# The first batch of an inducing-point attention and hard-swish kernel: a split first load, more input tiles in flight, weights cast while they are loaded, and a hand-written order for the first batch's coefficients

## The chip, the cores and the metric

One NeuronCore of a Trainium2 chip runs the kernel. Its engines are TensorE (PE, with its weight loads shown apart as PEld), VectorE (DVE), ScalarE (ACT), GpSimd (POOL) and SyncE (SP); SP and POOL issue the DMA transfers here. The metric is the device time of one execution in microseconds (us); lower is better. Executions of this kernel agree within about half a per cent.

## The reference

Four batches of N = 12480 tokens with C = 128 channels first meet m = 32 inducing points, then the tokens attend back, and the result runs through a two-layer block with a hard-swish.

```python
def mab(q, kv):
    s = scale * (q @ kv.transpose(0, 2, 1))
    s = s - s.max(-1, keepdims=True)
    a = np.exp(s)
    a /= a.sum(-1, keepdims=True) + 1e-09
    return a @ kv
h = mab(I, x)                    # 32 rows for each batch
x = mab(x, h).reshape(B * N, C)  # 49920 tokens
h = x @ w_in                     # d_ff = 2048
g = h * np.clip(h + 3.0, 0.0, 6.0) / 6.0
out = g @ w_out                  # float32, 49920 x 128
```

## The kernel before

The kernel never forms the 2048-wide hidden layer for each token. A token after the second attention is a weighted mean of the 32 rows of H (the `h` above), with weights that sum to one. As long as no entry of H @ w_in exceeds 3 in size, the hard-swish is a quadratic, and the square of a weighted mean is the weighted mean of the squares less a sum over pairs of rows: weight of m times weight of n times the squared difference. So each batch needs 32 x 128 linear coefficients (`L`, spread over a block-diagonal tile `BD`) and 512 x 128 pair coefficients (`Cq`), and each token needs its 32 exponentials and the 512 products of two of them. A counter at the end checks that the shortcut held; otherwise a slow direct path runs.

The tokens of a batch are cut into seven groups: six of 2048 (128 partitions with 16 tokens each, 1 MB) and a last one of 192 (48 partitions with 4 tokens). A group has four chunks of 512 tokens, the last group one, so a batch has 25 chunks.

The work of a batch has three stages, named by the first letter of the functions.

Stage a gathers H: `load_x` brings a group in from DRAM on the POOL queue (float32 for the matmuls, tiles `xr`, four of them), `a_cast` makes a bf16 copy `xb` on ACT and DVE, `a_T` transposes it on PE into `pt` in two halves and DVE copies each half to `xT`, `a_s1` computes the scores `s` and ACT takes the exponential `a`, `a_agg` adds a'x into one PSUM bank `hnd` and DVE adds `a` into `dacc`. At the end of a group's `a_agg` the load of the group four further on is issued, and for the first batch the load of the two weight matrices goes out after that of its last group.

Stage c makes the coefficients: `c_sum` and `c_den` reduce `dacc` and normalise `hnd` to H, `c_HT` transposes H and forms the differences `dH` and sums `W`, `c_sq` squares dH'w_in in 16 blocks, `c_C` multiplies these with w_out into `cp`, `c_G`, `c_hs`, `c_L` and `c_BD` make the linear part, and `c_tail` copies `cp` to `Cq`. Both need w_in and w_out in bf16 as well as in float32: before the change w_in is cast in two halves on ACT (lines 630 and 637) and w_out is scaled by -1/6 on DVE (line 641).

Stage b works on chunks. `b_pack` and `b_e` make a group's exponentials, `b_spread` copies rows of `dk` across partitions with a DMA on the SP queue into `d`, `b_base` and `b_prod` make the pair terms `TF` and `TD`, `b_f` and `b_r` the normaliser, `b_lin` and `b_quad` multiply with `BD` and `Cq` into `op`, and `b_evac` scales to `os`, from which SP writes the output.

Every engine works through its instructions in the order in which the program writes them. That order is written by hand: the loop over chunks (lines 666 to 714) emits stage b of chunk t and prepares chunks t+1 to t+5; between its pieces `bg` takes units of stages a and c of the next batch from a queue at an even rate. The first batch has nothing to hide behind: `a_first` emits its stage a (lines 291 to 308), then the first units of stage c with filler matmuls (`warm`) between them, and the rest of stage c runs in five steps of the loop with t below zero, beside the preparation of the first chunks.

```python
queue = c_units(0)
...
n_units, span = len(queue), (LEAD + 3)
begin = -LEAD - 3
for t in range(-LEAD - 3, total):
```

Of the kernel before, what the change touches and what calls it, by code (L numbers as in the profile page):

```python
# [9 lines left out]
FP32 = mybir.dt.float32  # L10
FP32R = mybir.dt.float32r
BF16 = mybir.dt.bfloat16
# [14 lines left out]
XBUF = 4  # L27
# [12 lines left out]
def kernel(  # L40
# [38 lines left out]
    with ExitStack() as es:  # L79
# [3 lines left out]
        xin = es.enter_context(tc.tile_pool(name="xin", bufs=XBUF))  # L83
        xbin = es.enter_context(tc.tile_pool(name="xbin", bufs=2))
# [20 lines left out]
        def load_x(b, g):  # L105
            t0, p, n = groups[g]
            src = x[b, t0 : t0 + p * n, :].rearrange("(p i) c -> p i c", i=n)
            t = xin.tile([P, TG, C], FP32R, name="xr")
            nc.gpsimd.dma_start(t[:p, :n, :], src)  # L109
            xs[(b, g)] = t  # L110
        for g in range(XBUF):
            load_x(0, g)
# [6 lines left out]
        ones = const.tile([P, P], FP32, name="ones")  # L119
        nc.vector.memset(ones[:, :], 1.0)  # L120
        blk_f = const.tile([P, P], FP32, name="blk_f")
        nc.vector.memset(blk_f[:, :], 0.0)
        one4_f = const.tile([P, SL], FP32, name="one4_f")
        nc.vector.memset(one4_f[:, :], 0.0)
        for q in range(4):
            nc.vector.memset(blk_f[32 * q : 32 * q + 32, 32 * q : 32 * q + 32], 1.0)
            nc.vector.memset(one4_f[32 * q : 32 * q + 32, q : q + 1], -1.0)
        blk = const.tile([P, P], FP32R, name="blk")
        nc.vector.tensor_copy(blk[:, :], blk_f[:, :])
        one4 = const.tile([P, SL], FP32R, name="one4")  # L130
        nc.vector.tensor_copy(one4[:, :], one4_f[:, :])
# [3 lines left out]
        nc.vector.tensor_copy(sel[:, :, :], ident[:M, :M].unsqueeze(1).to_broadcast([M, 4, M]))  # L135
        sel = sel[:, :, :].rearrange("k q m -> k (q m)")


        i_of = const.tile([P, 1], I32, name="i_of")
        nc.gpsimd.iota(i_of[:, :], pattern=[[0, 1]], base=0, channel_multiplier=1)  # L140
        nc.vector.tensor_single_scalar(i_of[:, :], i_of[:, :], 3, op=ALU.bitwise_and)
        half_of = const.tile([P, 1], FP32, name="half_of")
        nc.vector.tensor_copy(half_of[:, :], i_of[:, :])
# [86 lines left out]
        def a_agg(b, g, h, a1):  # L230
# [665 lines left out]
```

## Time and profile before

| | |
|---|---|
| Time, median of 3 runs | 333.91 us (332.82 to 334.44) |
| Profiled execution, own time | 333.31 us |
| Its span, from the first to the last recorded instruction | 331.5 us |
| PE busy | 300.7 us (91% of the span) |
| DVE, ACT, POOL busy | 242.1, 228.2, 17.7 us |
| Mean granted TensorE clock | 0.98 |
| HBM read, written | 27.67 MB, 25.56 MB |

The page gives one profiled execution, times in microseconds from the span's start. A busy PE is not PE at its peak, because matmuls are pipelined. Each row of a group of instructions names the line, the engine, the operation, what it writes and reads, the shapes and the count, then its busy time and the mean of one in ns, then the idle time ahead of it and what ended that. In the timeline the columns are start, duration (of all instructions in a merged row), engine, line and names. In the chain of waits, work is followed back from the last instruction to what released it. In a table of stretches each engine has its busy time and count, then the granted clock (1.00 is full), the share of time that the DMA engines were busy and the rate in GB/s.

### The profile page before, as it was taken

Reading aid. Unit: us, or ns where it says so; the run is one execution under the profiler, and the core shown is the slowest. Engines: PE = TensorE matmul, PEld = TensorE weight load, DVE = VectorE, ACT = ScalarE, POOL = GpSimd, SP = SyncE. Lnnn points to the kernel's source line nnn. Section 1 sums busy time; section 2 is a strip of 40 time slices with the busy share of each in tenths; the row PEclk is TensorE's granted clock in tenths of the full one; section 3 lists DMA queues with packets and bytes.
Section 4 is the critical chain, followed back from the end, with each engine's and each line's share of the span. In section 5 each row is a group of like instructions: output and inputs, shape, how many; then the busy total and the mean of one; then the engine's idle time right before and its main releaser. Section 6 shows DMA issues by size and latency. Waiting matters only on the chain.

```text
span 331.5 us, 9598 instructions
## 1 busy us (share of the span) xinstructions
PE 300.7 (91%) x3926; PEld 236.3 (71%) x3926; DVE 242.1 (73%) x560; ACT 228.2 (69%) x412; POOL 17.7 (5%) x37
## 2 busy tenths in 40 slices
PE   0868878999999998999999998999999999999970
PEld 0757456888767786888767886888767787777760
DVE  4765757778786866877795866878795867887980
ACT  2442459888579758888479758888479656777720
POOL 3031100001100000010100000010000000000000
PEclk9998979999999999999999999999999999999996
DMA  7699930378895455478994446473644356666561
GB/s 257 253 320 329 371 72 18 81 223 288 292 397 182 129 167 183 109 237 289 318 398 146 102 164 198 130 235 133 187 162 162 73 167 189 189 219 205 192 243 42
DMA packets 24134, 66.73 MB, mean 201 GB/s; under 512 B 3056, under 2 KB 17424, under 8 KB 17808
## 3 DMA queue, kind: packets, MB, share of 16 engines
q1 hardware_dynamic: 18160, 38.36, 35.7%
q0 software_dynamic: 5920, 27.66, 25.9%
q8 instruction: 33, 0.54, 0.7%
q14 instruction: 21, 0.17, 0.1%
HBM read 27.67 MB, written 25.56 MB: 161 GB/s over the span
## 4 chain that ended last, share of the span: by engine, by line
PE 80%; DVE 8%; ACT 5%; issue 2%; DMA 2%; POOL 1%; POOLq 0%; DVEq 0%
PE op L591 27%; PE bp L551 12%; PE hnd L235 7%; PE op L575 6%; PE pt L213 6%; PE dpm L414 4%; PE cp L434 4%; PE s L221 3%; PE pp L522 2%; DVE xT L214 2%; DMA xr<-in_x_dram 2%; PE sp L492 2%; PE lp L388 1%; PE ep L478 1%; ACT xb L204 1%
## 5 line engine op out<-in xcount | busy, mean ns | idle before, releaser
L558 ACT ACTIVATE TF<-bp 128x512 bf16<-128x512 f32 (+1 forms) x200 | 118.7, 601 | 35.0 <-PE rp L511 18.2
L591 PE MATMUL op<-Cq,TF 128*128 128x128 bf16 (+1 forms) x800 | 109.7, 223 | 0.2 <-DVE Cq L447 0.2
L591 PE MATMUL op<-Cq,TD 128*128 128x128 bf16 (+1 forms) x800 | 106.5, 219 | 0.0
L607 DVE TENSOR_TENSOR os<-op,r_all 128x512 f32<-128x512 f32 (+1 forms) x100 | 68.3, 683 | 21.0 <-PE op L591 19.9
L551 PE MATMUL bp<-xT,W 128*128 128x512 bf16 (+1 forms) x200 | 75.1, 376 | 0.0
L591 PEld LDWEIGHTS <-TF 128*128 128x128 bf16 (+1 forms) x800 | 50.4, 98 | 34.0 <-issue 25.5
L567 DVE TENSOR_TENSOR TD<-TF,d 128x1024 bf16<-128x1024 bf16 (+1 forms) x100 | 66.8, 668 | 3.9 <-ACT TF L558 2.1
L591 PEld LDWEIGHTS <-TD 128*128 128x128 bf16 (+1 forms) x800 | 61.5, 98 | 0.2 <-issue 0.2
L575 PE MATMUL op<-BD,nf 128*128 128x512 f32 (+1 forms) x100 | 52.9, 529 | 0.0
L204 ACT CAST xb<-xr 128x1024 bf16<-128x1024 f32 (+1 forms) x49 | 46.5, 957 | 8.0 <-DMA xr<-in_x_dram 7.8
L214 DVE COPY xT<-pt 128x1024 bf16<-128x1024 bf16 (+1 forms) x56 | 34.3, 618 | 12.2 <-PE pt L213 12.0
L425 ACT ACTIVATE sq<-dpm 128x512 bf16<-128x512 f32 x60 | 36.2, 651 | 6.0 <-PE dpm L414 5.9
L235 PE MATMUL hnd<-xr,a 128*32 128x128 f32 (+1 forms) x400 | 35.5, 231 | 1.7 <-ACT a L227 1.6
L213 PE MATMUL pt<-ident_b,xb 128*128 128x128 bf16 (+1 forms) x400 | 33.0, 229 | 4.1 <-DVE xb L204 4.1
L512 DVE RECIPROCAL r_all<-rp 128x4 f32<-128x4 f32 (+1 forms) x100 | 17.7, 177 | 23.0 <-PE rp L511 22.8
L511 PE MATMUL rp<-one,nf 128*128 128x4 f32 (+1 forms) x100 | 34.5, 345 | 0.0
L227 ACT ACTIVATE a<-s 128x512 fp32r<-128x512 f32 (+1 forms) x28 | 15.4, 551 | 22.4 <-PE s L221 17.7
L235 PEld LDWEIGHTS hnd<-xr,a 128*32 128x32 f32 (+1 forms) x400 | 27.1, 112 | 4.8 <-ACT a L227 2.9
L213 PEld LDWEIGHTS <-xb 128*128 128x128 bf16 (+1 forms) x400 | 25.7, 103 | 6.4 <-DVE xb L204 4.2
L109 POOL DMA_DIRECT2D xr<-in_x_dram x28 | 15.1, 542 | 205.2 <-PE bp L551 135.1
L434 PE MATMUL cp<-w6n,sq 128*128 128x128 bf16 x256 | 24.4, 220 | 1.0 <-DVE BD L408 1.0
L414 PE MATMUL dpm<-dH,w_in_b 128*128 128x512 bf16 x64 | 24.1, 389 | 0.9 <-ACT w_in_b L637 0.6
(99 smaller groups left out, 333.4 us busy)
## 6 DMA issues: line engine op xcount, KB each, us to landing
xr<-in_x_dram POOLq DMA_DIRECT2D x24, 1024.0 KB, 6.7
out_dram<-os SPq DMA_DIRECT2D x24, 1024.0 KB, 4.1
d<-dk SPq DMA_DIRECT2D x96, 128.0 KB, 3.9
w_in_r<-in_moe_w_in_dram POOLq DMA_DIRECT2D x1, 1024.0 KB, 6.1
w_out_r<-in_moe_w_out_dram POOLq DMA_DIRECT2D x1, 1024.0 KB, 10.2
xr<-in_x_dram POOLq DMA_DIRECT2D x4, 96.0 KB, 5.4
out_dram<-os SPq DMA_DIRECT2D x4, 96.0 KB, 1.9
d<-dk SPq DMA_DIRECT2D x4, 48.0 KB, 3.9
```

Of the source, the lines that this page charges most:

```text
L204: eng(xb[:p, lo:hi, :], xs[(b, g)][:p, lo:hi, :].bitcast(FP32))
L213: nc.tensor.transpose(pt[:, (i - lo) * p : (i - lo + 1) * p], xb[:p, i, :], ident_b[:p, :p])
L214: nc.vector.tensor_copy(st["xT"][:, t0 + lo * p : t0 + hi * p], pt[:, : (hi - lo) * p])
L235: nc.tensor.matmul(st["hnd"][:M, :C], lhsT=a1[:p, i * M : (i + 1) * M], rhs=xs[(b, g)][:p, i, :], start=(g == 0 and i == 0), stop=(g == NG ...
L414: nc.tensor.matmul(dpm[:, :], lhsT=w_in_b[:, jb * P : (jb + 1) * P], rhs=st["dH"][:, :, :, :, :].rearrange("p q k m i -> p (q k m i)"),)
L434: nc.tensor.matmul(st["cp"][:, k * C : (k + 1) * C], lhsT=sq[:, k * P : (k + 1) * P], rhs=w6n[:, jc, :], start=(jc == 0 and k == 0), stop= ...
L551: nc.tensor.matmul(bp[:, :w], lhsT=st["W"][:, k].rearrange("p m i -> p (m i)"), rhs=st["xT"][:, c0 : c0 + w],)
L558: nc.scalar.activation(st[("x", c)][:, k, :w], bp[:, :w], ACT.Exp, scale=scale)
L567: nc.vector.tensor_mul(u[:, :, :w], t[:, :, :w], d[:, :w].unsqueeze(1).to_broadcast([P, 2, w]))
L575: nc.tensor.matmul(op[:p, :], lhsT=st[("nf", g)][:, j * p : (j + 1) * p], rhs=st["BD"][:, :], start=True, stop=False, skip_group_check=True,)
L591: nc.tensor.matmul(op[:p, s * C : (s + 1) * C], lhsT=T[k][:, s * p : (s + 1) * p], rhs=st["Cq"][:, k, :], start=False, stop=(s == SL - 1 a ...
L607: nc.vector.tensor_mul(ot[:p, j * SL : (j + 1) * SL, :], op[:p, :].rearrange("p (s c) -> p s c", c=C), r_all[:p, b, c, :].unsqueeze(2).to_ ...
```

## The change

Five things change, all but the last two only for the first batch.

The first group is loaded in two halves; the loads of groups 1 to 4 follow behind the making of `ident` on POOL, and five `xr` tiles are there in place of four. The last, small group has a tile of its own (`xl`). The loads of the second batch's first five groups are held back until the copy `d` of the first batch's chunk 3 has landed (`load_held`).

The two weight matrices are each loaded twice, once with a cast to bf16 in the transfer and once in float32; they are issued after the first batch's last group. The casts on ACT and the scaling on DVE go; the factor -1/6 moves to `c_tail`.

The constants that DVE made at the start are made on POOL, behind the first five loads; filler matmuls on a zero tile run on PE at the start.

In `a_first`, ACT casts three quarters of a group and DVE one quarter, both halves of the transposes come ahead of the previous group's `a_agg`, and the last small group's sums no longer go through `dacc`. A hand-written function `c_first` takes the place of the queue for the first batch's stage c and of the loop's steps below zero; the casts of the second batch's first group move into step 0.

The later batches' units change a little: three empty units after `c_HT` in place of one, `c_C` starting after 12 of the 16 `c_sq`, and four empty units ahead of the second batch's. The pools for `TF`, `TD`, `e`, `nf` and `sq` have other sizes.

```diff
-XBUF = 4
+XBUF = 5
+SQB = 12
...
-        efp = es.enter_context(tc.tile_pool(name="efp", bufs=3))
+        efp = es.enter_context(tc.tile_pool(name="efp", bufs=2))
+        nfp = es.enter_context(tc.tile_pool(name="nfp", bufs=3))
...
-        tp = es.enter_context(tc.tile_pool(name="tp", bufs=LEAD + 2))
+        tf = es.enter_context(tc.tile_pool(name="tf", bufs=LEAD + 1))
+        td = es.enter_context(tc.tile_pool(name="td", bufs=LEAD))
...
-        sqp = es.enter_context(tc.tile_pool(name="sqp", bufs=FB))
+        sqp = es.enter_context(tc.tile_pool(name="sqp", bufs=SQB))
...
-        for g in range(XBUF):
-            load_x(0, g)
+
+        load_x(0, 0, 2)
+
+        held = []
+
+        def load_held(c, n):
+
+            seen = cst.tile([P, 1], BF16, name="seen")
+            nc.gpsimd.tensor_copy(seen[:, :], S[0][("d", c)][:, 0:1])
+            for _ in range(n):
+                load_x(1, held.pop(0))
+
+        def load_next(b, g):
+
+            if g < XBUF and g + XBUF < NGR:
+                load_x(b, g + XBUF)
+            elif b == 0:
+                held.append(g - (NGR - XBUF))
+            elif b + 1 < B:
+                load_x(b + 1, g - (NGR - XBUF))
...
+        def load_weights():
+            w_out = moe_w_out.rearrange("(kb kp) c -> kp kb c", kp=P)
+            nc.gpsimd.dma_start(w_in_b[:, :], moe_w_in[:, :])
+            nc.gpsimd.dma_start(w_in_r[:, :], moe_w_in[:, :])
+            nc.gpsimd.dma_start(w_out_b[:, :, :], w_out)
+            nc.gpsimd.dma_start(w_out_r[:, :, :], w_out)
...
+        for g in range(1, XBUF):
+            load_x(0, g)
+        wake = const.tile([P, 512], BF16, name="wake")
+        nc.vector.memset(wake[:, :], 0.0)
...
+        warm(4)
...
+        warm(8)
+
+        eng = nc.gpsimd
...
+        eng.memset(blk_f[:, :], 0.0)
...
+            eng.memset(t[:, :].bitcast(FP32), 0.0)
...
             else:
-                ahead = g + XBUF
-                if ahead < NGR:
-                    load_x(b, ahead)
-                if b == 0 and ahead == NGR - 1:
+                load_next(b, g)
+                if b == 0 and g == NGR - XBUF - 1:
                     load_weights()
-                if ahead >= NGR and b + 1 < B:
-                    load_x(b + 1, ahead - NGR)
...
-            both = ((nc.vector.tensor_copy, 0, 2), (nc.scalar.copy, 2, 4))
-            a_cast(0, 0, both)
+            both = ((nc.scalar.copy, 0, 2), (nc.scalar.copy, 2, 3), (nc.vector.tensor_copy, 3, 4))
+            a_cast(0, 0, ((nc.scalar.copy, 0, 2), (nc.vector.tensor_copy, 2, 4)))
             late = None
             for g in range(NGR):
                 if g + 1 < NGR:
                     a_cast(0, g + 1, both)
                 a_T(0, g, 0)
+                a_T(0, g, 1)
                 if late:
                     a_agg(0, g - 1, 0, late)
-                a_T(0, g, 1)
-                if late:
                     a_agg(0, g - 1, 1, late)
                 a_s1(0, g)
                 late = S[0]["a1"]
+            half_rows()
...
-            nc.vector.tensor_copy(Cq[:, 0:3, :].rearrange("p k c -> p (k c)"), cp[:, : 3 * C])
+            nc.vector.tensor_scalar_mul(Cq[:, 0:3, :].rearrange("p k c -> p (k c)"), cp[:, : 3 * C], -1.0 / 6.0)
...
+        def c_first():
+
+            c_sum(0)
+            c_sum(0, False)
+            warm(2)
+            c_den(0)
+            warm(3)
+            c_HT(0)
+            warm(4)
+            sq = lambda *jbs: [c_sq(0, jb) for jb in jbs]
+            cs = lambda *jcs: [c_C(0, jc) for jc in jcs]
+            sq(0, 1, 2)
+            b_pack(0, 0)
+            b_e(0, 0)
+            for c in range(4):
+                b_spread(0, c)
+            load_held(3, len(held))
+            for jb in range(3, 7):
+                sq(jb)
+                c_G(0, 4 * jb - 12, 4 * jb - 8)
+                cs(jb - 3)
+            c_hs(0)
+            sq(7)
+            cs(4)
+            b_f(0, 0)
+            sq(8)
+            b_base(0, 0, 0)
+            b_base(0, 0, 1)
+            cs(5)
+            c_L(0, 0)
+            c_L(0, 1)
+            sq(9)
+            cs(6)
+            b_prod(0, 0)
+            sq(10)
+            cs(7)
+            c_BD(0)
+            sq(11)
+            cs(8)
+            b_base(0, 1, 0)
+            b_r(0, 0)
+            for jb in range(12, FB):
+                sq(jb)
+                cs(jb - 3)
+            b_base(0, 1, 1)
+            cs(13, 14, 15)
+            c_tail(0)
+            b_pack(0, 1)
+            b_e(0, 1)
+            c_max(0)
...
-        queue = c_units(0)
-        half = FB // 2 * P
-        queue.pop(0)()
-        nc.scalar.copy(w_in_b[:, :half], w_in_r[:, :half].bitcast(FP32))
...
-        nc.scalar.copy(w_in_b[:, half:], w_in_r[:, half:].bitcast(FP32))
...
-        nc.vector.tensor_scalar_mul(w6n[:, :, :], w_out_r[:, :, :].bitcast(FP32), -1.0 / 6.0)
+        c_first()
+        queue = []
...
-        for t in range(-LEAD - 3, total):
+        for t in range(total):
...
-                    queue += a_units(b + 1) + c_units(b + 1)
+                    queue += ([lambda: None] * 4 if b == 0 else []) + a_units(b + 1) + c_units(b + 1)
```

More of the change, by code (lines that the diff above doesn't have):

```diff
@@ new lines @@
+        w_in_b = const.tile([P, F], BF16, name="w_in_b")
+        w_in_r = const.tile([P, F], FP32R, name="w_in_r")
+        w_out_b = const.tile([P, FB, C], BF16, name="w_out_b")
+        w_out_r = const.tile([P, FB, C], FP32R, name="w_out_r")
+        def load_weights():
[4 more added lines that the diff above has]
+            nc.gpsimd.dma_start(w_out_r[:, :, :], w_out)
@@ L154, with warm @@
-        nc.vector.memset(d_all[:, :], 1.0)
+        def warm(n):
+            wp = psF.tile([P, 512], FP32, name="wp", tag="fb")
+            for _ in range(n):
+                nc.tensor.matmul(wp[:, :], lhsT=wake[:, :P], rhs=wake[:, :])
+        warm(4)
         I_T = const.tile([P, M], BF16, name="I_T")
@@ L319, in c_sum @@
             )
[L320 removed]
+            st["dred"] = st.get("dred", []) + [dred[:p, :]]
         def c_den(b):
@@ L384, in c_L @@
             if h == 0:
-                st["lp"] = psH.tile([P, 512], FP32, name="lp", tag="hnd")
+                st["lp"] = (psH if b else psF).tile([P, 512], FP32, name="lp", tag="hnd" if b else "fb")
             lp = st["lp"]
@@ L436, in c_C @@
                     lhsT=sq[:, k * P : (k + 1) * P],
-                    rhs=w6n[:, jc, :],
+                    rhs=w_out_b[:, jc, :],
                     start=(jc == 0 and k == 0),
```

176 lines of the change are left out of this document (80 added, 96 removed).

## The prediction

> **What bounds the kernel now.** I read the page first, then a table of stretches that cuts the span where its stages change, then the timeline and the chain of waits of the first stretch. Table of stretches (columns: stretch, length, busy time and count of PE, PEld, DVE, ACT, POOL, granted clock, DMA share, GB/s):
>
> ```profile
> 0.00:6.50 6.50, 0.31 (x1) 0.18 (x1) 1.97 (x20) 1.28 (x1) 3.08 (x11) 1.00 0.61 210
> 6.50:33.50 27.00, 20.36 (x301) 18.03 (x302) 17.68 (x34) 10.56 (x15) 4.89 (x8) 0.94 1.02 310
> 33.50:38.00 4.50, 3.94 (x19) 1.51 (x19) 3.08 (x8) 1.68 (x4) 0.61 (x2) 1.00 1.04 397
> 38.00:54.30 16.30, 14.29 (x138) 9.72 (x138) 11.21 (x21) 10.72 (x21) 0.00 (x0) 0.90 0.34 108
> 54.30:331.50 277.20, 261.83 (x3474) 206.90 (x3471) 208.13 (x481) 203.99 (x373) 9.08 (x17) 0.99 0.60 193
> ```
>
> The last stretch is the loop from step 0 on; PE is busy in 94% of it. The 54.3 us ahead of it have PE busy for 38.9 (0.31 + 20.36 + 3.94 + 14.29), and nearly all of the change lies there: stage a of the first batch until 33.5, H and the differences until 38, the coefficients until 54.3. Loads first, from two tables of stretches (PE, clock, DMA share, GB/s) and from the timeline:
>
> ```profile
> 11.00:12.00 1.00, 0.78 (x14) 1.00 1.06 426
> 13.00:14.00 1.00, 1.00 (x12) 1.00 0.21 74
> 14.00:15.00 1.00, 1.00 (x19) 1.00 0.00 0
> 20.00:22.00 2.00, 0.69 (x13) 1.00 1.00 381
> 25.00:26.00 1.00, 1.00 (x12) 0.50 1.04 377
> ...
> 6.52 1.04 ACT L204 CAST xb<-xr 128x1024 bf16<-128x1024 f32 x1 [4.48 <-DMA xr<-in_x_dram]
> 9.00 0.69 DVE L204 CAST xb<-xr 128x1024 bf16<-128x1024 f32 x1 [0.51 <-DMA xr<-in_x_dram]
> ```
>
> Four loads of 1.05 MB run at 426 GB/s until 13.2, and then nothing is in flight: the fifth needs a buffer. Groups 0 and 1 reach their casts at 6.52 and 9.00, 2.48 apart, which is 1.05 MB / 426 GB/s = 2.46. The fifth load is the one long wait in the chain of waits, PE starves behind it (0.69 us of work in 2), and at 25 its clock is granted at half. Pieces of that chain, with the later ones that the change touches (start, length, what):
>
> ```profile
> 15.36 5.24 DMA xr<-in_x_dram
> ...
> 51.60 0.93 ACT xb L204
> ...
> 54.81 1.10 ACT xb L204
> ```
>
> When loads are there, a group takes 3.2 us, exponential to exponential. Timeline of group 5:
>
> ```profile
> 27.25 0.60 ACT L227 ACTIVATE a<-s 128x512 fp32r<-128x512 f32 x1 [2.14 <-PE s L221]
> ...
> 28.44 0.62 PE L213 MATMUL pt<-ident_b,xb 128*128 128x128 bf16 x8
> 29.31 0.68 DVE L214 COPY xT<-pt 128x1024 bf16<-128x1024 bf16 x1
> ...
> 30.45 0.60 ACT L227 ACTIVATE a<-s 128x512 fp32r<-128x512 f32 x1 [2.32 <-PE s L221]
> ```
>
> In the program the second half of the transposes (28.44) stands behind the first half of `a_agg`, and that behind the previous exponential. So the first stage has two limits, the missing buffer and this loop of dependences.
>
> **The change, term by term.** I move four marks of the execution shown: end of stage a, the first `dpm`, the first `op` of the loop, the end. Their rows, and the prices of a group's work:
>
> ```profile
> 33.07 0.42 PE L235 MATMUL hnd<-xr,a 48*32 48x128 f32 x4 [0.36 <-ACT a L227]
> 33.37 1.06 DVE L314 TENSOR_REDUCE dred<-dacc 128x32 f32<-128x512 f32 x1
> 37.94 0.38 PE L414 MATMUL dpm<-dH,w_in_b 128*128 128x512 bf16 x1 [0.56 <-ACT w_in_b L637]
> 54.30 0.58 PE L575 MATMUL op<-BD,nf 128*128 128x512 f32 x1
> ...
> L246 DVE TENSOR_TENSOR dacc<-dacc,a 128x512 f32<-128x512 f32 x5 | 3.4, 684 | 0.3 <-ACT a L227 0.3
> ...
> 59.25 0.45 PE pt L213 x8
> 60.84 0.48 PE hnd L235 x8
> 63.89 0.39 PE s L221 x16
> ```
>
> *Stage a: -6.5 us.* With five tiles, and a sixth load that needs only group 0's `a_agg` (about 13.0 in the new order), the transfers run on without a gap: group g reaches its cast at 6.5 + 2.46 g, group 5 at 18.8. Work for one group is then ACT 1.04 + 0.52 + 0.60 = 2.16, DVE a quarter cast of 0.35 + 2 x 0.69 + 0.68 = 2.41, PE 2 x 0.45 + 2 x 0.48 + 0.39 = 2.25: each just under 2.46. Both transposes now precede `a_agg`, so the loop of dependences no longer holds an exponential between the halves. The halved first load helps little: its cast begins at about 5.3, but DVE's quarter cast of group 1, which stands ahead of the copies to `xT`, waits for 9.0 anyway. Followed through from group 5: casts 19.1 to 20.7 behind group 3's exponential, transposes until 21.9, copies 21.4 to 22.8 behind `dacc`, scores and exponential until 23.9, `a_agg` until 24.9, the small group's scores, exponential and `a_agg` until 26.0. With three engines this close to the pace I add 1.0 for hand-overs: 27.0, against 33.07 + 0.42 = 33.5. Bounds: 26.0, and 30.0 if the period stays at 3.2 (group 0's exponential at 11.2, that is 9.0 + 0.35 + 2 x 0.69 + 0.39 and the hand-over; 5 x 3.2; and 2.8 as above from group 5's exponential to the end).
>
> POOL's added setup is some 19 instructions; from the row of the BD fill on DVE (0.49) and twice that on POOL I take 5 us, 5.3 to 10.3, covered by the wait for group 0. At three times that, the sixth load would go out at 20 and land 5.24 later, 6.7 after 18.8.
>
> *H and differences: -0.4.* 33.5 to 37.94 is 4.45. The big `dred` no longer waits for the small group, whose own reduction is a quarter of 1.06 (0.3); the copy to `d_all` (0.15) goes behind H; no `w_in_b` cast holds the first `dpm`. I take 4.05. The first `dpm` then stands at 31.0.
>
> *Coefficients: -1.2.* Prices for this stage, by group and from the chain:
>
> ```profile
> L425 ACT ACTIVATE sq<-dpm 128x512 bf16<-128x512 f32 x12 | 7.0, 600 | 5.1 <-PE dpm L414 5.0
> L641 DVE TENSOR_SCALAR w6n<-w_out_r 128x2048 bf16<-128x2048 f32 x1 | 1.2, 1227 | 0.0
> L173 DVE MEMSET BD<- 128x512 f32 x2 | 1.0, 485 | 0.1
> ...
> 47.34 0.22 PE dpm L414
> 47.55 0.22 PE cp L434 x4
> 51.12 0.49 ACT sq L425
> 38.31 1.69 PE gp L362 x16
> 42.16 1.88 PE lp L388 x16
> ```
>
> PE: 16 x (0.22 + 0.22) + 1.69 + 1.88 + about 2.5 for the first chunks (eleven matmuls at 0.22 by the `dpm` row) = 13.1; ACT: 12 squares at 0.49, eight exponentials at about the same and two copies to BD (0.5 together, an estimate) = 10.3. From 37.94 to 54.30 were 16.36, with two casts (0.93 and 1.10) on the chain and DVE's 1.23 for `w6n`; these leave. Followed by hand, counted from the first `dpm`: `gp` done +4.8, `hs` +6.5 behind a square on DVE, `lp` +8.3, `lt` +9.6, the four copies to BD, in turn ACT and DVE, +11.8, and ACT's last three squares and two exponentials after them +14.3; last `cp` +14.4, `Cq` +15.2. So 15.2 in place of 16.4, between 13.1 and 16.4. First `op` of the loop: 46.2 against 54.3.
>
> Held loads: they wait for `d` of chunk 3, issued near 33.
>
> ```profile
> 41.40 3.76 SPq L538 DMA_DIRECT2D d<-dk  x4
> 57.80 0.37 PE L221 MATMUL s<-I_T,xT 128*128 128x32 bf16 x8 [0.98 <-DVE xT L214]
> 21.72 0.58 POOL L167 DMA_DIRECT2D w_in_r<-in_moe_w_in_dram  x1
> ...
> w_in_r<-in_moe_w_in_dram POOLq DMA_DIRECT2D x1, 1024.0 KB, 6.1
> w_out_r<-in_moe_w_out_dram POOLq DMA_DIRECT2D x1, 1024.0 KB, 10.2
> ```
>
> 33 + 3.8 + 5.24 = 42, and step 0 casts that group at 46: hidden, with 4 us to spare; POOL holds nothing else then.
>
> *Weights.* Issued behind the last group, w_in, issued at 21.72, lands 6.1 later at 27.8 now, and w_out, issued 0.58 behind it, 10.2 later at 32.5: 4.7 us for its 1.05 MB in 512 B pieces, 223 GB/s. No row casts to a narrower type in a transfer. At these steps, from 18.4 on: `w_in_b` about 21, `w_in_r` 23.5, `w_out_b` 28.2, `w_out_r` 33, against first uses at 31, 32, 33 and 37.6: nothing, down to 4.6 us of slack. From below it can't gain; from above it is the second rival.
>
> By the Trainium skill's page "DMA: Bandwidth & Descriptors", section Specifications, pieces under 512 B pay a read-modify-write; `w_out_b` is written in 256 B pieces. The rows agree in direction (4.7 us for 512 B pieces); twice 4.7 for `w_out_b` would put `w_out_r` at 38.3 and the sum 0.7 higher, at 325.2.
>
> *Loop: -0.7.* Step 0 has PE idle for 0.98 before `s`; the second batch's units now start four units later and that wait goes, while its two casts (2.0 on ACT) come into the step: -0.7, between -1.5 and +1. The smaller rings cost nothing: the exponential that refills a `TF` follows a `bp` which PE runs after the matmuls that free it, and `b_prod` stands on DVE behind `b_evac`, which waits for those that free `TD`. `cp` holds one of five PSUM banks for four blocks longer in three batches, which I price at one 512-column matmul (0.22) each time, within the bounds.
>
> By the Trainium skill's page "SBUF — State Buffer", section Who interferes with whom, a DVE cast in a two-port mode and a POOL instruction exclude each other; by that rule DVE's two casts before 10 wait up to 1 us together, ahead of a load that comes later anyway, and the sum stays.
>
> Sum against the execution's own 333.31 (331.5 and 1.8 around it): 333.3 - 6.5 - 0.4 - 1.2 - 0.7 = **324.5 us**. That execution lies 0.6 below the median of 333.91, inside the runs' 332.82 to 334.44. No change means within 0.5% (1.67 us) of 333.91, about what can be told here.
>
> **Rivals.** *The engines pace, not the loads.* Everything is in flight but a group still takes 3.2. For it: three engines have work of 2.2 to 2.4 in a pace of 2.46, in fixed order. Against it: the exponential leaves the loop of dependences. Stage a ends at 30.0: 327.5.
>
> *The casting loads are slow (slower than before).* Place: `c_L` waits for `w_out_r`, last of four. Price: with k times the steps above for the two casting loads (7.2 together), `w_out_r` lands at 26 + 7k, and what follows `c_L` takes 8.7 more, so `op` starts at 35 + 7k; it hurts from k = 1.6, reaches 54.3 at 2.8 and is slower beyond 3. At k = 4: 333.3 + 8.7 - 0.7 = 341. For it: no row of such a transfer, 2048 pieces; against it: the float32 load of the same 2048 pieces takes 4.7 us, and a narrower type writes half the bytes.
>
> *The loads are not all in flight.* POOL's setup delays the sixth load by 6.7 as priced, and the change does not do what it says: 331.
>
> *The loop gives it back.* The longer-held bank and the squeezed units of the second batch cost 0.1 us in each of 75 steps that have background work: 332 to 334, no change.
>
> **How the numbers follow.** Load-paced, as forecast, 0.58, its own range 322 to 327; engine-paced 0.22; sixth load late 0.08; loop 0.06; slow casts 0.06. Low end 320.5: stage a at 26.0, coefficients at 13.1 and loop at -1.5 (-1.0 - 2.1 - 0.8 = -3.9). High end 330 takes in the engine-paced case; left out are the slow casts, the loop, and half of the late load. Faster 0.58 + 0.22 + 0.06 = 0.86, no change 0.08, slower 0.06.
>
> **What will show it.** Exponentials of stage a 2.5 to 2.7 apart (3.2: first rival); ACT's casts ended by loads 2.46 apart, and a DMA rate above 400 GB/s from 4 to 18 without a hole; full clock from 7 on; first `dpm` near 31, not waiting for `w_in_b`; no wait of `cp` or `lp` for a weight; first `op` near 46; 277 us from there to the end. A first `op` after 52, or a loop longer than 279, makes the prediction wrong.

## The result, and the profile after

The changed kernel takes 325.31 us (median of four runs, 323.27 to 330.37) beside 334.03 for the kernel before on the same chip (332.82 to 334.44). The ratio is 0.972, 95% interval 0.966 to 0.979; undisturbed executions alone enter every ratio here. The profiled execution took 323.27, 10.0 less than the 333.31 of the one shown of before. Table of stretches of the changed kernel, cut at the same four marks (columns as before):

```profile
0.00:6.50 6.50, 5.02 (x13) 1.53 (x13) 0.69 (x3) 2.13 (x2) 5.17 (x25) 1.00 0.65 187
6.50:28.40 21.90, 17.71 (x301) 16.41 (x302) 16.57 (x32) 12.02 (x20) 6.83 (x14) 0.84 1.10 332
28.40:31.65 3.25, 2.72 (x15) 0.98 (x16) 2.35 (x9) 0.27 (x2) 0.00 (x0) 1.00 2.39 311
31.65:45.61 13.96, 13.28 (x137) 9.10 (x138) 9.80 (x21) 10.10 (x21) 2.86 (x6) 1.00 0.64 192
45.61:321.50 275.89, 261.10 (x3475) 206.68 (x3471) 208.13 (x481) 204.88 (x373) 8.48 (x16) 0.99 0.62 202
```

Cut at the exact marks, the gain is 5.1 in stage a (33.49 to 28.38), 1.2 in H and the differences (4.45 to 3.27), 2.4 in the coefficients (16.36 to 13.96) and 1.3 in the loop (277.2 to 275.9). The last two hang on the mark: `Cq` is written from 0.17 after the first `op` before (54.47) and from 0.48 ahead of it now (45.13), so counted from `Cq` the coefficients gain 3.05 and the loop 0.66. That execution is the fastest of the four. From its chain of waits:

```profile
3.00 6.84 DMA xr<-in_x_dram
...
13.65 1.71 PE hnd L282 x16
15.36 0.46 PE s L268 x16
15.82 0.08 issue
15.89 5.32 DMA xr<-in_x_dram
```

and the marks in its PE timeline:

```profile
27.96 0.42 PE L282 MATMUL hnd<-xl,a 48*32 48x128 f32 x4 [0.36 <-ACT a L274]
31.65 0.81 PE L470 MATMUL dpm<-dH,w_in_b 128*128 128x512 bf16 x3 [0.53 <-DVE dH L400]
38.02 1.15 PE L444 MATMUL lp<-w_out_r,hs 128*32 128x128 f32 x16
45.61 0.58 PE L676 MATMUL op<-BD,nf 128*128 128x512 f32 x1
```

Two loads stand in the chain: group 1's, issued at 3.00, and the sixth, issued at 15.89, which waits for a buffer until group 0's `a_agg` has run. The first `dpm` waits for DVE, not for `w_in_b`. Loads and clock in stage a, from tables of 2 us:

```profile
8.00:10.00 2.00, 1.03 (x8) 0.77 (x8) 0.90 (x2) 0.13 (x1) 0.80 (x3) 0.71 1.07 422
10.00:12.00 2.00, 0.84 (x19) 0.74 (x20) 1.49 (x3) 1.45 (x3) 0.00 (x0) 0.50 1.05 418
12.00:14.00 2.00, 2.00 (x22) 2.00 (x20) 1.35 (x3) 2.00 (x3) 0.00 (x0) 0.50 1.09 438
14.00:16.00 2.00, 2.00 (x36) 1.96 (x35) 1.14 (x3) 0.19 (x2) 0.11 (x1) 0.59 1.02 410
16.00:18.00 2.00, 2.00 (x47) 1.99 (x45) 1.70 (x3) 1.89 (x3) 2.00 (x4) 1.00 0.68 135
```

The transfers run at 410 GB/s or more from 8 to 16, then fall to 135: the sixth load came just too late to keep them going. The granted clock is half from 8.8 to 15.6. Exponentials start at 11.98, 15.84, 18.11, 20.39, 23.32, 25.60 and 27.63: 2.28 apart where neither half clock nor a load holds them, against 3.2 before. The timeline has the setup on POOL, the DVE cast beside it, and the issues of the weights:

```profile
6.82 0.97 POOL L200 MEMSET BD<- 128x512 f32 x2
7.06 1.70 DVE L251 CAST xb<-xr 128x1024 bf16<-128x1024 f32 x1 [3.41 <-DMA xr<-in_x_dram]
8.18 0.62 POOL L214 IOTA i_of<- 128x1 int32 x1
...
16.95 0.57 POOL L149 DMA_DIRECT2D w_in_b<-in_moe_w_in_dram  x1
17.52 0.54 POOL L150 DMA_DIRECT2D w_in_r<-in_moe_w_in_dram  x1
18.04 1.24 POOL L151 DMA_DIRECT2D w_out_b<-in_moe_w_out_dram  x1
19.27 1.15 POOL L152 DMA_DIRECT2D w_out_r<-in_moe_w_out_dram  x1
```

and the page's list of DMA issues has their time to landing in its last column:

```profile
d<-dk SPq DMA_DIRECT2D x96, 128.0 KB, 4.1
...
w_in_r<-in_moe_w_in_dram POOLq DMA_DIRECT2D x1, 1024.0 KB, 10.1
w_out_r<-in_moe_w_out_dram POOLq DMA_DIRECT2D x1, 1024.0 KB, 14.4
w_in_b<-in_moe_w_in_dram POOLq DMA_DIRECT2D x1, 512.0 KB, 6.8
w_out_b<-in_moe_w_out_dram POOLq DMA_DIRECT2D x1, 512.0 KB, 12.3
```

`w_in_b` lands at 23.8 (16.95 + 6.8) for a use at 31.65, `w_out_r` at 33.7 for a use at 38.02: no matmul waits for a weight.

### The profile page after: what moved, and what is told of

Read it like the earlier page. It is cut to its first block, busy times and chain, and to the rows that moved or that the text cites. A ratio compares the mean times of both kernels' runs of the same rounds, so it can differ in the third digit from the quotient of the medians.

```text
span 321.5 us, 9629 instructions
## 1 busy us (share of the span) xinstructions
PE 299.8 (93%) x3934; PEld 234.7 (73%) x3934; DVE 237.5 (74%) x542; ACT 229.4 (71%) x416; POOL 23.3 (7%) x59
## 4 chain that ended last, share of the span: by engine, by line
PE 75%; DMA 11%; DVE 6%; ACT 3%; issue 2%; POOL 0%; DVEq 0%; POOLq 0%
PE op L692 26%; PE bp L652 12%; DMA d<-dk 8%; PE op L676 6%; PE hnd L282 6%; PE pt L260 5%; PE cp L490 4%; PE dpm L470 4%; DMA xr<-in_x_dram 4%; PE s L268 3%; PE pp L623 2%; DVE xT L261 2%; PE sp L593 2%; PE ep L579 2%; DVE TD L668 1%
## 5 line engine op out<-in xcount | busy, mean ns | idle before, releaser
L659 ACT ACTIVATE TF<-bp 128x512 bf16<-128x512 f32 (+1 forms) x200 | 117.9, 600 | 34.8 <-PE rp L612 21.2
L260 PE MATMUL pt<-ident_b,xb 128*128 128x128 bf16 (+1 forms) x400 | 31.0, 223 | 2.0 <-DVE xb L251 1.5
L282 PE MATMUL hnd<-xr,a 128*32 128x128 f32 x384 | 31.8, 229 | 0.5 <-ACT a L274 0.5
L282 PEld LDWEIGHTS hnd<-xr,a 128*32 128x32 f32 x384 | 25.6, 111 | 2.7 <-issue 2.1
L260 PEld LDWEIGHTS <-xb 128*128 128x128 bf16 (+1 forms) x400 | 24.6, 100 | 3.9 <-DVE xb L251 1.6
L118 POOL DMA_DIRECT2D xr<-in_x_dram x25 | 13.5, 543 | 161.8 <-ACT TF L659 94.4
L490 PE MATMUL cp<-w_out_b,sq 128*128 128x128 bf16 x256 | 24.3, 220 | 0.4 <-ACT sq L481 0.4
L630 ACT ACTIVATE dk<-pp 128x512 bf16<-128x512 f32 (+1 forms) x28 | 15.8, 564 | 11.5 <-PE pp L623 10.5
```

Source lines behind the costliest of these rows:

```text
L260: nc.tensor.transpose(pt[:, (i - lo) * p : (i - lo + 1) * p], xb[:p, i, :], ident_b[:p, :p])
L282: nc.tensor.matmul(st["hnd"][:M, :C], lhsT=a1[:p, i * M : (i + 1) * M], rhs=xs[(b, g)][:p, i, :], start=(g == 0 and i == 0), stop=(g == NG ...
L490: nc.tensor.matmul(st["cp"][:, k * C : (k + 1) * C], lhsT=sq[:, k * P : (k + 1) * P], rhs=w_out_b[:, jc, :], start=(jc == 0 and k == 0), s ...
L659: nc.scalar.activation(st[("x", c)][:, k, :w], bp[:, :w], ACT.Exp, scale=scale)
```

## The experiments

All experiments compute the whole output; each is the changed kernel with one edit, or with several where it says so. "Stage a ends" is the end of the last `a_agg`. The stages are read from the one profiled execution of each kernel. Its time also holds what happened in the loop, which differs by several microseconds from one execution to the next (experiment 9), so a time alone doesn't give the worth of an edit in the first batch.

**1. The old order of a group.** Back to `a_agg` between the halves of the transposes.

```diff
                 a_T(0, g, 0)
-                a_T(0, g, 1)
                 if late:
                     a_agg(0, g - 1, 0, late)
+                a_T(0, g, 1)
+                if late:
                     a_agg(0, g - 1, 1, late)
```

> The changed kernel with one thing undone: in the first batch's stage a, the first half of a_agg again stands between the two halves of the transposes. My theory: the loop of dependences through the exponential is what made a group take 3.2 us once its load was there, and the new order removes it; so the period goes from 2.28 (exponentials at 15.84, 18.11, 20.39) to about 3.2 in the three stretches that no load holds, stage a ends about 2.5 us later (near 30.9 in place of 28.4) and the time is 326 to 327.5 where the changed kernel has 324.5. Rival: the loads set the pace and the order is worth nothing; then stage a ends within 0.5 us of 28.4.

329.26 us, ratio 0.987 (0.981 to 0.993). Stage a ends at 30.62, 2.2 later, with exponentials in its timeline 2.97 apart:

```profile
18.67 0.60 ACT L274 ACTIVATE a<-s 128x512 fp32r<-128x512 f32 x1 [0.92 <-PE s L268]
21.64 0.60 ACT L274 ACTIVATE a<-s 128x512 fp32r<-128x512 f32 x1 [0.92 <-PE s L268]
24.61 0.60 ACT L274 ACTIVATE a<-s 128x512 fp32r<-128x512 f32 x1 [0.92 <-PE s L268]
```

The order brings a group from 2.97 to 2.28. Undone, it gives the engine-paced rival, and the changed kernel is not it; of the 5.1 that stage a gained, 2.2 are the order's.

**2. Four tiles.** `XBUF = 4`.

> The changed kernel with four large input tiles in place of five. Theory of the missing buffer: the fifth load then waits for group 0's a_agg (15.9) and lands at 21.2, the sixth for group 1's and lands near 24.3; stage a ends about 3 us later than 28.4, the time is about 327. Rival: since the fifth tile lets only one load more go out early and the sixth waits until 15.9 anyway, the hole in the transfers only moves by one group and stage a ends less than 1 us later.

330.97 us, ratio 0.994 (0.992 to 0.996). Now two loads wait for buffers (issued at 15.37 and 17.87) and stage a ends at 31.7, 3.3 later. So the fifth tile is worth 3.3, and what is left without it, 1.8, is near the order's 2.2: the two nearly add.

**3. Fillers around group 0.** Six extra matmuls on `wake` behind each half of group 0's transposes.

> The changed kernel with six filler matmuls more behind each half of group 0's transposes, so that PE has work between 7.4 and 10.9. Theory: in the changed kernel the granted clock is half from 8.8 to 15.6, group 0's a_agg ends at 15.4 rather than near 13, and the sixth load, which waits for it, goes out at 15.9 and lands at 21.2; with the clock kept up a_agg ends near 13.6, the sixth load lands near 19, stage a ends about 2 us earlier (26.4) and the time is 1.5 to 2.2 us below the changed kernel's, 322.5. Rival: the clock does not decide, since the loads come only every 2.5 us; then nothing moves by more than 0.5.

324.9 us, ratio 0.975 (0.970 to 0.981), as the changed kernel. The clock stays full through stage a and the sixth load goes out at 14.21 in place of 15.89, yet stage a ends at 28.15, 0.2 earlier, as the rival had it: group 5 is cast by DVE at 21.03, as before (21.23). The half clock is real, but it was hidden.

**4. Loads 1 to 4 ahead of the identity's setup.**

> The changed kernel with the loads of groups 1 to 4 issued ahead of the identity on POOL, as before the change. Theory: in the changed kernel groups 1 to 3 reached their casts at 9.87, 12.49 and 14.93, 0.9 later than the kernel before would have had them, because their loads were issued from 3.0 on and the transfers ran at 279 GB/s from 4 to 5; with the loads first the casts start at about 9.0, 11.5 and 13.9. The sixth load still waits for group 0's a_agg, which then ends some 0.5 earlier: stage a ends 0.5 us earlier, the time is about 324. Rival: the late identity holds the first transposes and the end of stage a stays or goes up by 0.5.

329.06 us, ratio 0.988 (0.984 to 0.992): slower than the changed kernel. The theory fell, and the rival's 0.5 was too small: group 1 reached its cast at 9.86, exactly as before (9.87), so the time of issue is not what sets the landing. Group 5 came at 22.14, PE ran dry behind it, the clock was halved from 24.0 to 27.3, and stage a ended at 30.76, 2.4 later.

**5. Setup back on DVE** (only the iota stays on POOL).

```diff
-        eng = nc.gpsimd
+        eng = nc.vector
```

> The changed kernel with the constants made on DVE again (only the iota stays on POOL). In the changed kernel DVE's cast of group 0's second half took 1.70 us where the same cast took 0.63 before, while POOL filled BD beside it. Theory: the two engines shut each other out, and with POOL idle the cast takes 0.6 to 0.7 again; it is hidden, because the copies to xT wait for group 1's load (9.87), so stage a ends where it did (28.4, give or take 0.5 and what the clock does). Rival: the cast is on the path, stage a ends 1 us earlier; or the cast stays at 1.7, and it was not POOL.

Two runs, 324.5 and 331.06 us. Its DVE timeline has the cast of 1.70 above at its usual length:

```profile
7.11 0.69 DVE L251 CAST xb<-xr 128x1024 bf16<-128x1024 f32 x1 [0.76 <-DMA xr<-in_x_dram]
```

Stage a ends at 28.68 all the same: the scores of group 0 stand behind DVE's quarter cast of group 1, whose load lands at 9.8. The reverse shows in the kernel with a sixth tile (experiment 8): there DVE's cast starts at 7.13 and takes 0.69, and POOL's cast of `blk` beside it, from 7.26, takes 0.70 in place of 0.29.

**6. Float32 weights only, narrow copies cast by ACT and DVE.**

```diff
-            nc.gpsimd.dma_start(w_in_b[:, :], moe_w_in[:, :])
...
-            nc.gpsimd.dma_start(w_out_b[:, :, :], w_out)
...
             c_sum(0, False)
+            nc.scalar.copy(w_in_b[:, :half], w_in_r[:, :half].bitcast(FP32))
             warm(2)
...
+            nc.scalar.copy(w_in_b[:, half:], w_in_r[:, half:].bitcast(FP32))
+            nc.vector.tensor_copy(w_out_b[:, :, :], w_out_r[:, :, :].bitcast(FP32))
```

> The changed kernel with only the float32 loads of the weights, and the casts on ACT (two of 1.03) and DVE (one of 1.2) in the places where the kernel before had them. Theory: the casting loads save what lay on the path, the second w_in cast ahead of the first dpm and the 1.2 us on DVE ahead of the first square there: the stretch from the first dpm to Cq goes from 13.5 to 14 to 14.7 and the first dpm comes up to 0.5 later, 0.5 to 1.5 in all. Rival: the casts fit into idle time of ACT and DVE and cost less than 0.3, and the casting loads are worth nothing.

Two runs, 331.95 and 328.1 us, ratio 0.989 (0.981 to 0.997). The stretch that the casts touch hardly moves: 3.30 from stage a's end to the first `dpm` (3.27 with casting loads) and 13.73 from there to `Cq` (13.48). So in this one execution the rival holds: with the new order around them the engine casts cost 0.3 us on this stretch. What this execution lost beside that, it lost elsewhere: group 5 landed at 22.4, and one TD in the loop waited 3.56 for `d` (experiment 9).

**7. The old queue for the coefficients**, with casting loads kept: the units of stage c run between the steps -5 to -1, as before.

```diff
-        c_first()
-        queue = []
+        queue = c_first()
...
-        for t in range(total):
+        for t in range(-LEAD - 3, total):
```

> The changed kernel with the first batch's stage c in the order that the kernel before had, taken from the queue in five steps of the loop below zero, but with the weights from the casting loads. Theory: the hand-written order is worth most of what the stretch from the first dpm to Cq gained (16.5 before, 13.5 after): 15.5 to 16.5 here, so Cq comes 2 to 3 us later than in the changed kernel, counted from the first dpm. Rival: the gain came from the casts that left; then the stretch stays within 0.7 of 13.5.

Two runs, 331.64 (the profiled one) and 322.83 us, which is less than any run of the changed kernel; the times show no worth of the order. The stretch does: from the first `dpm` to `Cq` are 15.17 in place of 13.48, to `op` 15.0 in place of 13.96, between the theory's range and the rival's. The order written by hand is worth 1.7 of the 3.05 that `Cq` gained (16.53 before), and 1.0 of the 2.4 counted to `op`; about half of the rest can be `lp`, 1.88 at half clock before and 1.15 now.

**8. When does the sixth load land?** First the weights held back until group 5 is there, with the fillers of 3:

```diff
+            nc.gpsimd.tensor_copy(seen_x[:, :], xs[(0, 5)][:, 0, 0:1].bitcast(FP32))
             nc.gpsimd.dma_start(w_in_b[:, :], moe_w_in[:, :])
```

> The changed kernel with the fillers of e3_warm and with the weight loads held until group 5 has landed. In e3_warm the sixth load went out at 14.2 and reached its cast only at 21.2, and so did it in e4_loads (14.3 to 22.2), though nothing but the rest of group 4 was ahead of it. Theory: the four weight loads issued right behind it share the transfer engines with it and cost it 2 to 3 us; held back, it lands at about 18.7 to 19.3, the exponential of group 4 comes at about 18.9 to 19.5 in place of 20.7, stage a ends at about 26.3 (27.7 in e3_warm), the weights still land before they are used, and the time is 1 to 1.5 us below e3_warm's. Rival: a load issued at 14.2 takes 7 us there whatever follows it; then stage a ends at 27.7 and the later weights cost time.

324.13 to 330.12 us over four runs. Issued at 14.72, group 5 is cast by DVE at 21.34 with no weight in flight (the first goes out at 21.75), and stage a ends at 28.47; the 27.7 of the expectation is the start of the last `a_agg`, not its end. The theory that the weights delay it fell. DVE's timeline has the casts of groups 3, 4 and 5:

```profile
15.34 0.43 DVE L253 CAST xb<-xr 128x512 bf16<-128x512 f32 x1 [0.50 <-DMA xr<-in_x_dram]
18.70 0.43 DVE L253 CAST xb<-xr 128x512 bf16<-128x512 f32 x1 [1.14 <-DMA xr<-in_x_dram]
21.34 0.43 DVE L253 CAST xb<-xr 128x512 bf16<-128x512 f32 x1 [0.41 <-DMA xr<-in_x_dram]
```

Group 4, asked for at 4.6 with the others, is itself late: it comes 3.4 behind group 3 where the pace until then was 2.5, and group 5 comes 2.6 behind it. So the pace was lost ahead of the sixth load, before any weight was asked for. Experiments 3 and 10 have the same step, group 4 at 18.4 and 18.7.

Then a sixth tile, borrowed from the output tiles, so that nothing waits for a buffer:

```diff
-                t = xin.tile([P, TG, C], FP32R, name="xr")
+                pool, key = (osp, "os") if (b, g) == (0, XBUF) else (xin, "xr")
+                t = pool.tile([P, TG, C], FP32R, name=key)
...
-        for g in range(1, XBUF):
+        for g in range(1, NGR):
             load_x(0, g)
```

> The changed kernel with a sixth full tile for the first batch (group 5 borrows an output tile that the loop does not need yet), so that all seven x loads of the batch are issued at the setup and none waits for a buffer. Theory (the sixth load starts late, 15.9 in place of 13, and is slow because it starts alone into an empty queue): group 5's cast by ACT moves from 21.3 to 18.8 to 19.5, stage a ends at 26.5 to 27.3 in place of 28.4, first op 44 to 45, 322 to 323.5. Rival (from group 2 on the engines and the half clock of that stretch pace stage a, period 2.27): group 5's data are there by 19, but its exponential comes no more than 0.4 us earlier, stage a still ends at 28 to 28.4 and the time stays at 323 to 325.

327.18 us, ratio 0.979 (0.975 to 0.983): not faster. Its timeline:

```profile
5.11 0.57 POOL L119 DMA_DIRECT2D os<-in_x_dram  x1
...
21.14 0.43 DVE L253 CAST xb<-os 128x512 bf16<-128x512 f32 x1 [1.08 <-DMA os<-in_x_dram]
```

and its table of stretches:

```profile
16.00:18.00 2.00, 2.00 (x46) 1.99 (x44) 1.97 (x4) 1.14 (x3) 0.00 (x0) 1.00 1.08 426
18.00:20.00 2.00, 2.00 (x47) 1.99 (x45) 1.83 (x3) 1.77 (x4) 0.00 (x0) 1.00 1.05 294
20.00:22.00 2.00, 1.82 (x32) 1.65 (x29) 0.92 (x3) 1.40 (x2) 0.00 (x0) 1.00 1.09 280
```

Issued ten microseconds earlier, group 5 lands at 21.1 again, so the theory missed; stage a ends at 28.28, within the rival's 28 to 28.4, but not for its reason, that the data are there by 19. In eight executions (the changed kernel, 3, 5, both of 8, 9, 10 and 11) group 5 is asked for between 5.1 and 15.9 and cast at 21.0 to 21.6, and stage a ends 7.1 later. In three more (4, 6 and 7, issued at 14.3 to 15.5) it is cast at 22.1 to 23.0, PE runs dry, half clock follows, and the end comes 8.2 to 8.6 later. So with five tiles or six the buffer no longer paces the stage; the landing does. Its cause stays open. With the sixth tile the weights were already in the queue and it moved only 294 and 280 GB/s from 18 on; with the weights held back the pace slipped at group 4 all the same. A sixth tile with the weights held back was not run.

**9. `d` ahead of the store of `out`.** In five profiled executions of these variants (3, 4, 6, 7 and the sixth tile) one TD between 85 and 91 us waited 2.6 to 3.6, and in experiment 2 one at 77.8 waited 2.7. In the loop DVE makes TD from `d`, which SP's queue spreads, and that queue also carries the 1 MB store. In the execution of the sixth-tile kernel, the timeline has:

```profile
73.66 0.35 SPq L717 DMA_DIRECT2D out_dram<-os  x1
74.10 7.19 SPq L641 DMA_DIRECT2D d<-dk  x4
...
82.33 0.60 ACT L661 ACTIVATE TF<-bp 128x512 bf16<-128x512 f32 x1 [0.26 <-PE bp L654]
85.91 0.69 DVE L670 TENSOR_TENSOR TD<-TF,d 128x1024 bf16<-128x1024 bf16 x1 [3.11 <-ACT TF L661]
```

and its table of stretches:

```profile
86.00:88.00 2.00, 0.30 (x3) 0.16 (x4) 1.97 (x5) 0.00 (x0) 0.00 (x0) 0.92 0.61 237
88.00:90.00 2.00, 1.98 (x15) 1.51 (x16) 1.66 (x6) 0.60 (x1) 0.00 (x0) 0.50 0.42 172
```

The row puts the wait down to TF, but that TF was done at 82.9, 3 us before TD started; its other input is the `d` sent behind the store. PE has 0.30 us of work in the next 2, and then runs at half clock for 6.8 us. The cost shows in the loop's first batch, from `Cq` to `Cq`: in the six executions with such a wait it took 78.2 to 81.8 us, in the seven others, those of experiments 9 to 11 included, 74.5 to 77.5. The edit moves the spread ahead of the eviction, so that the chunk behind the store is one that is needed a step later:

```diff
-            if evac:
-                b_evac(*evac)
-                evac = None
             if 0 <= t + 4 < total:
                 b_spread(*divmod(t + 4, NCK))
+            if evac:
+                b_evac(*evac)
+                evac = None
```

> The changed kernel with one edit in the loop: the rows of d for four chunks ahead are sent to SP's queue ahead of the eviction (and so ahead of the 1 MB store of out) instead of behind it. In the profiled execution of the changed kernel's variants DVE's TD waits 2.6 to 3.6 us for d where the store stands directly ahead of it (73.97, 11.26 us under way). Theory (the store ahead in the queue makes d late): no wait of TD for d above 1 us anywhere in the loop, no half clock behind one, fast runs within 322 to 325, ratio to the kernel before 0.966 to 0.974. Rival (the x loads that share the DMA engines make it late): waits of 2 to 4 us stay and the runs spread from 322 to 331 as before.

323.57 us (322.61 to 325.06, six runs), ratio 0.9705 (0.967 to 0.974), as the theory had it. Its DVE timeline at the same place:

```profile
83.00 0.68 DVE L668 TENSOR_TENSOR TD<-TF,d 128x1024 bf16<-128x1024 bf16 x1
86.39 0.69 DVE L668 TENSOR_TENSOR TD<-TF,d 128x1024 bf16<-128x1024 bf16 x1 [0.59 <-DMA d<-dk]
```

`d` behind the store still needs 11.8 us (issued 74.54, used 86.39), but only 0.59 of it is waited for, and no half clock follows. Against the changed kernel's own ratio the intervals overlap, so a gain in the median isn't shown; in this execution the loop's first batch took 75.2, where the changed kernel's had 74.5 with no late `d` in it. The runs lie closer together, 2.5 us over six here and 2.3 over six in experiment 10, where the four of the changed kernel span 7.1; so few runs don't settle that. Nor is the rival excluded as a part of the cause: the piece behind the store was as slow as ever with the loads of x running, and the edit only gave it more time.

**10. Sixth tile, fillers and `d` first, together.**

> The sixth tile, the twelve extra fillers around group 0's transposes, and d ahead of the store of out, together. Theory (late d, the late sixth load and the half clock of the first stage are separate costs): stage a ends at 25.5 to 26.8, no TD wait above 1 us for d, 320.5 to 322.5, ratio 0.961 to 0.967. Rival (stage a is paced by its engines, and the loop's waits do not come from the store): 323 to 325, as the changed kernel.

323.83 us (322.37 to 324.68), ratio 0.9694 (0.966 to 0.973): the rival's 323 to 325. Stage a ends at 28.45, no better than alone; TD waits at most 0.58 for `d`. Beside the sixth tile alone (327.18) the two other edits take off 3.4 us, none of it in stage a, where the fillers act; that leaves `d`, but the two were not tried one by one with the sixth tile.

**11. One block of background units behind HT**, as before the change, in place of three. This line belongs to the change's edits for the later batches, which the diff above leaves out.

```diff
-            us = [lambda: c_sum(b)] + gap + [lambda: c_den(b)] + gap + [lambda: c_HT(b)] + 3 * gap
+            us = [lambda: c_sum(b)] + gap + [lambda: c_den(b)] + gap + [lambda: c_HT(b)] + gap
```

> The changed kernel with one block of background units instead of three behind the second and third batch's HT, as in the kernel before, so that the new third of that spacing alone is undone. Theory (the spacing is what made these two batches 0.4 us shorter each): Cq to Cq of a batch goes back from 73.6 to 74.0 and the time from first op to the end from 275.9 to 276.7. Rival (it does not matter; the smaller rings, the longer-held bank or the new order within a group did it): 73.6 stays within 0.15.

326.5 us, two runs. `Cq` of two batches in the timeline, first of this kernel:

```profile
196.26 0.53 DVE L503 TENSOR_SCALAR Cq<-cp 128x384 bf16<-128x384 f32 x1
270.08 0.53 DVE L503 TENSOR_SCALAR Cq<-cp 128x384 bf16<-128x384 f32 x1
```

and of the changed kernel:

```profile
193.72 0.53 DVE L503 TENSOR_SCALAR Cq<-cp 128x384 bf16<-128x384 f32 x1
266.89 0.53 DVE L503 TENSOR_SCALAR Cq<-cp 128x384 bf16<-128x384 f32 x1
```

73.82 against 73.17 in the loop's third batch. In the twelve executions that keep the spacing this stretch is 73.14 to 73.25, and before the change it was 73.99: here the spacing is worth 0.65 of 0.82. In the second batch it doesn't show as plainly: 73.85 without it, 74.05 in the changed kernel, where a TD waited 0.95 for `d`, and 73.17 and 73.16 in experiments 9 and 10, which also keep it and where none waited. In the first batch `dpm` waited 1.8 for `dH` without the spacing, half clock followed from 90.7 to 94.1, and the batch took 77.5 in place of 74.5. So from the first `op` to the end were 278.8 us, 2.9 more than in the changed kernel and 2.1 more than the theory had.

## Why the prediction was right, and where its steps were not

The time lies inside the range, 0.8 above the number; the terms were -6.5, -0.4, -1.2 and -0.7, measured -5.1, -1.2, -2.4 and -1.3. The measured terms belong to an execution 2.0 below the median; errors of both signs made the sum better than its parts. That the number came so close is in part luck: the four runs span 323.3 to 330.4.

*Stage a, -6.5: right in kind, 1.4 too much.* Load-paced was the forecast, and the landing of the last large load does set the end: in eight executions it follows group 5's cast by 7.1 (experiment 8), for which the prediction's walk gives 7.2 (18.8 to 26.0). In between, groups 2 and 3 went at the engines' 2.28, catching up after the half clock. The mis-sized term is "6.5 + 2.46 g, group 5 at 18.8": it came at 21.2. Group 1 was already 0.9 late (9.87 against 9.0), and from 16 on the transfers ran below their rate; why is not shown. The 1.0 for hand-overs was not needed, which took back part of the 2.4. "A sixth load that needs only group 0's `a_agg` (about 13.0)" failed as well, by 2.9: PE waited for group 0's cast and then got half clock, so that the `hnd` of group 0 ended at 15.36. Experiment 8 shows that this cost nothing: with the sixth load out at 5.1, stage a ended 0.1 earlier. "Full clock from 7 on", and no hole in the transfers before 18, were both wrong; the exponentials, given as 2.5 to 2.7 apart, were 2.3 where nothing held them, 3.9 at the half clock and 2.9 where the sixth load was awaited.

*The rivals.* Engine-paced was refuted by the period of 2.28, and experiment 1 shows what it would have been (2.97). The late sixth load came about by another way than POOL's setup, which took 3.7 (5.1 to 8.8) in place of 5 (the two fills of BD took 0.97, no longer than on DVE, where the prediction had doubled them), and was harmless. Slow casting loads: `w_out_b`, with pieces of 256 B, lands 2.7 after the load ahead of it (27.6 to 30.3), and float32 `w_out_r` 3.3 after that (30.3 to 33.7). By the Trainium skill's page "DMA: Bandwidth & Descriptors", section Specifications, those short pieces should have paid a read-modify-write; the doubling of 4.7 us that the prediction made of this did not come, and a smaller price can't be told from these rows. Nor does its 38.3 follow from its own steps: `w_out_r` at 33 and 4.7 later is 37.7, which would have put the sum 0.1 higher, not 0.7.

*POOL and DVE.* The second cast of group 0 took 1.70 beside POOL's fills, 0.69 without them (experiment 5). This is the mutual exclusion of the Trainium skill's page "SBUF — State Buffer", section Who interferes with whom; the trace agrees, with the 1.0 us that the prediction allowed, and it was hidden behind group 1's load as it said.

*H and differences, -0.4: 0.8 too little.* It is not the removed casts (3.30 with engine casts, experiment 6). Counted from the end of stage a, the two traces have the last reduction done at 0.4 in place of 0.9, `dps` on PE at 0.5 in place of 1.3, and H's transpose `htp` at 1.6 in place of 2.7. So the big `dred` that no longer waits gave 0.6. Most of the rest appears on PE, where six and five fillers stood ahead of `dps` and `htp` before and two and three do now; the prediction put the fillers at nothing. No run changed them alone.

*Coefficients, -1.2: 1.2 too little.* The walk by hand to 15.2 put waits on ACT and DVE that did not come. PE is busy for 13.28 of 13.96, so the lower bound (PE's sum of 13.1) was the better guide. Of the 3.05 counted to `Cq`, 1.7 is the order (experiment 7); `lp` at full clock can account for 0.7 more; casting the weights in the loads, which names the change, is worth about 0.3.

*Loop, -0.7: right sign, wrong reasons.* It measured -1.3 from the first `op` and -0.66 from `Cq`. "Step 0 has PE idle for 0.98 before `s` [...] that wait goes": it did not, as the changed kernel's timeline shows.

```profile
46.92 2.00 ACT L251 CAST xb<-xr 128x1024 bf16<-128x1024 f32 x2
48.80 1.10 ACT L659 ACTIVATE TF<-bp 128x512 bf16<-128x512 f32 x2
49.45 0.69 DVE L668 TENSOR_TENSOR TD<-TF,d 128x1024 bf16<-128x1024 bf16 x1 [1.37 <-ACT TF L659]
...
51.41 0.36 PE L268 MATMUL s<-I_T,xT 128*128 128x32 bf16 x8 [0.92 <-DVE xT L261]
```

The casts hold TF, TF holds TD, and TD holds `xT`. The loop's first batch (`Cq` to `Cq`) went from 74.31 to 74.54, the second from 74.00 to 74.05, the third from 73.99 to 73.17. The gain came from the spacing of the later batches (experiment 11), which the prediction had not priced. The rival that the loop gives it back has a real mechanism, the late `d`, though not the one named: 0.95 and 1.57 waited in this execution, 3.1 in that of experiment 8.

## What to carry to other kernels

When a stage has a missing buffer and a loop of dependences, expect each edit to bring a part: undone alone, one cost 2.2 and the other 3.3 of the 5.1 us. Once both limits are gone, ask when the last load lands, and don't read that from its issue: issued between 5.1 and 15.9, the sixth landed at 21.0 to 21.6 eight times, and up to 23.0 in three others. In a stretch where one engine has most of the work, its sum is a better estimate than a schedule followed by hand; and a short transfer that is needed soon should not stand in a queue directly behind a large store while other loads run, where it was late some of the time.

## What the runs showed of the hardware

A wait of 3 us in the loop costs more than itself: after it the granted clock was 0.50 for 6.8 us in the kernel with the sixth tile, and the batch took 79.3 from `Cq` to `Cq` against 74.5. In experiment 11 a wait of 1.8 us was followed by half clock as well. The half clock is also not tied to one place: in stage a it was granted from 8.8 to 15.6 in the changed kernel, where PE had 1.0 us of work between 6 and 9, and in experiment 4, where PE was busy there and ran dry between 21 and 24, not until 24.0. Nor does the same idle stretch always bring it: with 2.7 us of work between 48 and 52 the changed kernel kept its clock, with 2.8 the kernel of experiment 10 had half from 53.2 to 56.6.

128 KB pieces of `d` land 4.1 us after issue by the median. Of the first pieces behind each 1 MB store in the changed kernel's execution, three took 7.6 to 9.4 with loads of x running, and the others 2.5 to 6.1, some of them with such loads too (4.4 for the one issued at 61.0); in experiment 9 the one named there took 11.8.
